# Unit 3's pieces begin after fifteen instead of twelve halves of unit 2's x products

## Chip, cores and metric

The kernel runs on one core of one Trainium2 chip. The metric is device time in microseconds (us) of one execution, lower is better. A measurement is the median of several executions; the profile is one further execution, recorded by the hardware profiler.

## What is computed

A gated linear recurrence is followed by a feed-forward block, all in float32. Cut to what matters:

```python
# q, k, v, a_re, a_im: (batch 4, heads 8, seq 768, head_dim 48)
a = (a_re + i*a_im) scaled so that its magnitude is at most 0.999
for t in range(768):                       # per batch and head, state 48 x 48, complex
    S = a[t][:, None] * S + outer(k[t], v[t])
    y[t] = q[t] @ real(S)
x = y laid out as (4*768, 8*48) = (3072, 384)
h = ((x @ w1) * (x @ w2)) @ w3             # w1, w2: 384 x 1024, w3: 1024 x 1024
out = h @ w_out                            # w_out: 1024 x 384
```

## The kernel before

The recurrence is turned into matrix products. The sequence is cut into **units** of 384 time steps, two for each batch element, eight in all (`NU = 8`), and each unit into three **chunks** of 128 steps (`UC = 3`, `C = 128`). For every unit, VectorE (DVE) and ScalarE (ACT) first prepare gates: logarithms and exponentials of the gate's magnitude, running products and sums over time (the scans, L628 and L687), sines and cosines. Gates multiply q and k into four tiles: `gR` and `k` (for k), `gA` and `q` (for q). Twelve DMA transfers (L736) then move these four into the layout that the scores need, `KL` and `QL`. The gates of unit u+1 are prepared while TensorE (PE) works on unit u. GpSimd (POOL) does nothing but check the weights and gates from the side, in a loop of its own.

PE's work on a unit's attention is a list of **pieces**:

- `tr`: three transposes of a chunk of `gR` (x = 0) or `k` (x = 1) into PSUM (`tp`, L766), then a copy to SBUF by ACT (`KT`, L768);
- `kv`: 24 products of a chunk's `KT` with v (L830), which DVE adds to the state (`T`, L836);
- `sc`: scores of four heads (L780), which DVE copies under the causal mask into `A` (L783); two pieces make a chunk;
- `y`: the chunk's output (L813), copied by ACT to `xT` (L815).

`tp`, `kv` and `y` take turns in two PSUM buffers. An odd unit such as unit 3 has these pieces:

```python
return [[("need", u), tr[0][0]], [tr[0][1]], [tr[1][0], kv[0]], [tr[1][1]], [kv[1]], sc[0], sc[1] + [y[0]],
        sc[2] + [y[1], y[2], ("end", u)]]                                    # L1196
```

The feed-forward work of the unit before is what PE does between the pieces. For unit 2 it is a list of 25 items: first 16 **halves** of the x products, in turn x @ w1 (L852 `m<-xT,w1s`, copied by ACT to `a`, L857) and x @ w2 (L852 `m<-xT,w2s`, multiplied with `a` by DVE into `ab`, L859), one pair for each of eight column blocks; then `sum` (four sums on DVE, `So`, L887); then the products with the fused output weights, in the order p1, p2, p4, p6, p7, p5, p3 (L912; a Strassen scheme of seven products, combined on DVE in L894 and by one ACT copy, L917), with `keep` (an ACT copy of part of `ab`, L878) after p7. The function that weaves the two lists is this one:

```python
def unit(u, rest, ahead):                                                    # L1226
    ...
    seq = [("begin", u)] + rest[:ahead]
    rest = rest[ahead:]
    p = pieces(u) + [[]]
    n = len(p)
    first = [i * (len(rest) - 2) // (n - 1) for i in range(n)] + [len(rest)]
    for i in range(n):
        seq += rest[first[i]:first[i + 1]] + p[i]
    return seq
```

So `ahead`, which comes from the list `AHEAD` at L432, says how many of the 25 items come before unit 3's pieces begin; the rest are spread evenly among them.

PE's order is this list. On ACT, DVE and the DMA-issuing SyncE (SP), the order is that of a planner (`run` and `fill`): after each PE item, it places gate operations of the next unit where its own clock says that they fit before the engine's next request by PE's list. [...] The gate operations of unit 4 that the prediction names are, in order: `gR` and `gA` (L717, L719, DVE), which release the `im` tile; the load of the new `im` (L512, SP); `im` times `gR` (L600, DVE); its square with a running maximum (L604, DVE, to `gZ` and `st_tan`); the logarithm of `gZ` (L586, ACT, `gZ<-gZ,consts`); a sum (L614, DVE); two exponentials and a copy (L586, ACT); a minimum (L625, DVE); and three scans (L628, DVE).

Of the kernel before, what the change touches and what calls it, by code (L numbers as in the profile page):

```python
# [376 lines left out]
def kernel(  # L377
# [51 lines left out]
    TT = S // 2  # L429
    UC = TT // C  # L430
    NU = 2 * B
    AHEAD = [0, 3, 12, 12] + [8] * (NU - 4)  # L432
    LO, HI = 32, D - 32
    PASS, WIDE, SCAN, LAND, SLACK, LATE, RING, LOOK, NEAR, EARLY = 1.17, 1.4, 1.05, 1.8, 0.7, 1.2, 8, 4.0, 4, 2
    LOOKS = 3
# [765 lines left out]
    def ffn(u, parts=1):  # L1201
        ab = [x for j in range(KF) for x in ffn_ab(u, j)]
        last = [(("o", "half")[parts - 1] if n == parts - 1 else "part", f) for n, f in enumerate(ffn_out(u, UC - 1, parts))]
        if u == 0:
            return ab + [(("part", "half")[n], f) for t in range(UC) for n, f in enumerate(ffn_out(u, t, parts))]


        def pair(*tiles):
            return [(f"p{p}", f) for p, f in zip((1, 2, 4, 6, 7, 5, 3), out_pair(tiles))]

        own, thirds = ((u, 0, False), (u, 1, False)), ((u - 1, UC - 1, True), (u, UC - 1, False))
        if u == 1:
            return ab + [("so", lambda: (out_sums(own), last[0][1]()))] + pair(*own)
        got = ab + [("sum", lambda: out_sums(own))] + pair(*own)
        if u % 2:
            return got + [("sum", lambda: out_sums(thirds))] + pair(*thirds)
        return got[:len(ab) + 6] + [("keep", lambda: keep(u))] + got[len(ab) + 6:]
# [8 lines left out]
    def unit(u, rest, ahead):  # L1226

        if u == 1:
            return [("begin", u)] + mixed([x for p in pieces(u) for x in p], rest, FILLS[1])
# [8 lines that stand above are left out]
# [175 lines left out]
    with tc.manual_schedule(engines={mybir.EngineType.PE}):  # L1413
# [30 lines left out]
        with tc.manual_schedule(engines={mybir.EngineType.Activation, mybir.EngineType.DVE, mybir.EngineType.Pool, mybir.EngineType.SP}):  # L1444
# [23 lines left out]
            for u in range(1, NU):  # L1468
                seq += unit(u, rest[HEAD:] if u == 1 else ffn(u - 1), AHEAD[u])
            seq += ffn(NU - 1)  # L1470
# [43 lines left out]
```

## Time and profile before

| | before |
|---|---|
| time, median of 3 | 552.43 us |
| range of the 3 | 551.7 to 552.54 us |
| profiled execution, its own time | 552.92 us |
| span in that profile | 551.1 us |
| PE busy | 521.0 us, 95% of the span |
| DVE busy | 372.6 us, 68% |
| ACT busy | 275.3 us, 50% |
| POOL busy | 358.0 us, 65% |
| granted PE clock, mean | 0.982 of full |

All times in the text count from the start of the span. Of the profile's views, the table of busy time gives each engine's share; the timeline lists instructions with start, duration, engine, line, operation, output and inputs, and in brackets the engine's idle time just before and what ended it; the chain of waits follows the end of the run back through whatever released each step; the table of windows gives busy time, granted PE clock (1.00 is full), DMA share and GB/s for chosen stretches. [...]the price of a piece is taken from one start to the next.

### The profile page before, as it was taken

To read this page: it belongs to the slowest core of one execution; us is meant where nothing else is said; L and a number is where in the kernel's file an instruction comes from. 1 tells how busy PE (TensorE), PEld (TensorE's weight loads), DVE (VectorE), ACT (ScalarE), POOL (GpSimd) and SP (SyncE) were. 2 spreads that over 40 slices of the span, in tenths; PEclk is the share of its full clock that TensorE was granted. 3 is DMA by queue.
4 is the path that set the end of the run, shared out by engine and by line. 5 is a ranking of instruction groups with operands and counts; after the bars stand their busy time and mean duration, and the time that the engine had idled before them with its cause. 6 is when DMAs were issued, how large, how long until landed. Compare 5 with 4: busy or idle time off the path is not lost.

```text
span 551.1 us, 13443 instructions
## 1 busy us (share of the span) xinstructions
PE 521.0 (95%) x5546; PEld 370.0 (67%) x5546; DVE 372.6 (68%) x553; ACT 275.3 (50%) x391; POOL 358.0 (65%) x425
## 2 busy tenths in 40 slices
PE   4689899989999999989999999999999999999995
PEld 2345575556756795669568985687569966795585
DVE  5999589775585677867977985687669751531152
ACT  5989766465543555746467426743494232111100
POOL 1000000188888788888998888988998888888100
PEclk9899899999999999989999999999999999999999
DMA  8997956966659835492889346935793173222001
GB/s 262 339 395 236 212 167 189 253 161 162 159 141 242 223 106 132 146 207 84 245 212 218 112 129 165 215 110 152 170 224 100 58 205 83 73 65 96 1 26 39
DMA packets 73510, 89.73 MB, mean 163 GB/s; under 512 B 31840, under 2 KB 63264, under 8 KB 72672
## 3 DMA queue, kind: packets, MB, share of 16 engines
q1 hardware_dynamic: 67360, 69.78, 48.2%
q0 software_dynamic: 6080, 19.01, 11.7%
q8 instruction: 45, 0.74, 0.6%
q14 instruction: 25, 0.20, 0.1%
HBM read 65.14 MB, written 4.72 MB: 127 GB/s over the span
## 4 chain that ended last, share of the span: by engine, by line
PE 67%; DVE 14%; DMA 8%; ACT 5%; issue 3%; SPq 1%; DVEq 0%; ACTq 0%
PE m L852 35%; PE p L912 14%; PE y L813 6%; PE sc L780 5%; PE o L948 3%; DMA im<-in_a_im_dram 2%; DMA QL<-q 2%; DMA raw<-in_w_dram 2%; DVE gZ L687 2%; PE kv L830 2%; PE tp L766 2%; ACT low L1002 1%; DVE So L887 1%; DMA out_dram<-ot 1%; ACT gZ L586 1%
## 5 line engine op out<-in xcount | busy, mean ns | idle before, releaser
L852 PE MATMUL m<-xT,w1s 128*128 128x384 f32 x384 | 134.5, 487 | 1.1 <-ACT xT L815 1.1
L852 PE MATMUL m<-xT,w2s 128*128 128x384 f32 x384 | 134.8, 487 | 0.0
L852 PEld LDWEIGHTS m<-xT,w1s 128*128 128x128 f32 x384 | 72.2, 190 | 48.9 <-ACT xT L815 1.7
L852 PEld LDWEIGHTS m<-xT,w2s 128*128 128x128 f32 x384 | 71.9, 190 | 47.8
L1069 POOL TENSOR_SCALAR look<-look 128x256 f32<-128x256 f32 (+1 forms) x84 | 86.7, 1032 | 7.3
L1050 POOL TENSOR_TENSOR seen<-seen,look 128x256 bf16<-128x256 bf16 (+1 forms) x84 | 80.9, 963 | 6.8
L859 DVE TENSOR_TENSOR ab<-m,a 128x384 f32<-128x384 f32 x64 | 35.2, 551 | 69.8 <-PE m L852 66.3
L857 ACT COPY a<-m 128x384 f32<-128x384 f32 x64 | 30.2, 473 | 95.1 <-PE m L852 95.1
L1034 POOL MEMSET seen<- 128x256 bf16 x1 | 0.3, 311 | 102.3 <-DVE w2s L1014 102.3
L1068 POOL TENSOR_SCALAR look<-look 128x256 f32<-128x256 f32 (+1 forms) x44 | 51.7, 1174 | 6.1 <-DMA look<-in_a_re_dram 2.8
L1066 POOL TENSOR_TENSOR look<-look 128x256 f32<-128x256 f32 (+1 forms) x72 | 48.6, 675 | 3.5 <-DMA look<-in_w_dram 1.7
L912 PE MATMUL p<-To,So 128*128 128x192 f32 x240 | 44.1, 332 | 0.0
L1045 POOL DMA_DIRECT2D look<-in_w_dram x56 | 33.1, 591 | 16.6 <-POOL seen L1050 16.6
L815 ACT COPY xT<-y 128x384 f32<-128x384 f32 x24 | 11.5, 478 | 60.2 <-PE y L813 60.2
L1071 POOL TENSOR_TENSOR look<-look 128x256 f32<-128x256 f32 (+1 forms) x44 | 38.1, 866 | 3.7
L912 PEld LDWEIGHTS p<-To,So 128*128 128x128 f32 x240 | 38.7, 190 | 2.2 <-issue 2.0
L768 ACT COPY KT<-tp 128x384 f32<-128x384 f32 x40 | 34.0, 857 | 11.9 <-PE tp L766 11.7
L813 PE MATMUL y<-A,V 128*32 128x128 f32 x768 | 39.8, 273 | 0.1
L783 DVE COPY_PREDICATED A<-mask,sc 128x512 f32<-128x512 uint8 x48 | 32.7, 733 | 6.4 <-PE sc L780 6.2
L813 PE MATMUL y<-QL,T 96*32 96x128 f32 x640 | 35.5, 272 | 0.8 <-issue 0.8
L813 PEld LDWEIGHTS y<-A,V 128*32 128x32 f32 x768 | 34.3, 110 | 2.1 <-issue 2.0
L1150 PE MATMUL f<-wo_s,w3s 128*128 128x384 f32 x96 | 35.6, 520 | 0.0
(129 smaller groups left out, 922.4 us busy)
## 6 DMA issues: line engine op xcount, KB each, us to landing
look<-in_w_dram POOLq DMA_DIRECT2D x56, 256.0 KB, 4.0
raw<-in_w_dram SPq DMA_DIRECT2D x6, 1024.0 KB, 10.7
KL<-gR SPq DMA_DIRECT2D x24, 192.5 KB, 4.6
KL<-k SPq DMA_DIRECT2D x24, 192.5 KB, 6.1
re<-in_a_re_dram SPq DMA_DIRECT2D x24, 192.0 KB, 4.4
im<-in_a_im_dram SPq DMA_DIRECT2D x24, 192.0 KB, 4.0
k<-in_k_dram SPq DMA_DIRECT2D x24, 192.0 KB, 8.1
q<-in_q_dram SPq DMA_DIRECT2D x24, 192.0 KB, 7.4
```

Source lines behind the costliest of these rows:

```text
L768: nc.scalar.copy(out=KT_t[u, c][:, :, :, x].rearrange("p h d f -> p f d h"), in_=tp.rearrange("p f (d h) -> p f d h", h=H))
L813: nc.tensor.matmul(out=o, lhsT=a, rhs=b, start=s0, stop=s1)
L852: nc.tensor.matmul(out=m, lhsT=w[:, j * P // WB, f, j * P % WB:j * P % WB + P], rhs=xT_t[u][:, f], start=(f == 0), stop=(f == KD - 1))
L859: nc.vector.tensor_tensor(out=ab_t[u][:, j], in0=m, in1=got[0], op=OP.mult)
L912: nc.tensor.matmul(out=m[p], lhsT=a[:, f], rhs=b[:, f], start=(f == 0), stop=(f == KH - 1))
L1045: nc.gpsimd.dma_start(out=got.bitcast(I32)[:, 0:group[2]], in_=group[1])
L1050: nc.gpsimd.tensor_tensor(out=seen[:, 0:n], in0=seen[:, 0:n], in1=x, op=OP.add)
L1066: tt(out=x, in0=x, in1=x, op=OP.mult)
L1068: ts(out=y, in0=x, scalar1=high, scalar2=None, op0=OP.is_le)
L1069: ts(out=x, in0=x, scalar1=low, scalar2=None, op0=OP.is_ge)
L1071: tt(out=x, in0=x, in1=y, op=OP.mult)
L1150: nc.tensor.matmul(out=sums[j], lhsT=w3_t[f][:, j * P:(j + 1) * P], rhs=w3_t["wo"][:, f], start=(f == 0), stop=(f == KF - 1))
```

## The change

One number changes: the fourth entry of `AHEAD`, that of unit 3, from 12 to 15.

```diff
-    AHEAD = [0, 3, 12, 12] + [8] * (NU - 4)
+    AHEAD = [0, 3, 12, 15] + [8] * (NU - 4)
```

By `unit`, 13 items are left for the weaving before, 10 after. PE's order from the thirteenth half on (halves counted from 0; `tr c,x`) becomes:

```text
before  h12 tr0,0 | h13 tr0,1 | h14 h15 tr1,0 kv0 | sum tr1,1 | p1 kv1 | p2 p4 sc0 | p6 sc1 y0 | p7 keep sc2 y1 y2 | p5 p3
after   h12 h13 h14 h15 tr0,0 | sum tr0,1 | p1 tr1,0 kv0 | p2 tr1,1 | p4 kv1 | p6 sc0 | p7 sc1 y0 | keep sc2 y1 y2 | p5 p3
```

The planner sees another list, so the built orders of ACT and DVE differ in this stretch too; those of SP and POOL are the same as before. From the thirteenth half of unit 2 to unit 3's last output (Ln, Exp, Copy: the gate operations on ACT, L586; check: L564; sq: L604; A: one mask copy, L783; scan: L628; `|` only parts the columns):

```text
ACT before  a(h12) KT KT a(h14) Ln gZ | KT KT U | Exp Exp Copy check xT check keep xT Ln xT
ACT after   a(h12) a(h14) Ln gZ | KT KT U KT KT | Exp Exp Copy check check xT keep xT Ln xT
DVE before  .. sq ab(h15) T So So So So T L614 | A A L625 U ot | A A scan scan U ot | A A scan
DVE after   .. sq ab(h15) So So So So T L614 T L625 U ot | A A scan U ot | A A scan | A A scan
```

No operation, transfer or buffer is added or removed.

## Prediction

> **What bounds the kernel now.** I read the page first, for the engine that sets the time; then the chain of waits around unit 3, for what PE hangs on there; then the timelines of PE and ACT, for the order in which things stand; last the table of windows, for the clock. The page:
>
> ```profile
> PE 521.0 (95%) x5546; PEld 370.0 (67%) x5546; DVE 372.6 (68%) x553; ACT 275.3 (50%) x391; POOL 358.0 (65%) x425
> ...
> PE 67%; DVE 14%; DMA 8%; ACT 5%; issue 3%; SPq 1%; DVEq 0%; ACTq 0%
> ```
>
> PE is the bound, so reordering its work is worth only the PE idle time that it adds or removes. After 150 us and before the last products, PE has one large hole, and it lies in the stretch that the change rearranges. PE's timeline:
>
> ```profile
> 236.60 0.49 PE L766 MATMUL tp<-ident,gR 128*128 128x128 f32 x3
> 237.02 0.88 PE L830 MATMUL kv<-vr,KT 128*32 128x48 f32 x48
> 240.27 0.55 PE L766 MATMUL tp<-ident,k 128*128 128x128 f32 x3 [2.37 <-ACT KT L768]
> ```
>
> PE waits 2.37 us for an ACT copy out of PSUM. The chain of waits for that stretch says why the copy is late:
>
> ```profile
> 230.51 4.42 DMA im<-in_a_im_dram
> ...
> 235.04 1.40 DVE im L600
> ...
> 238.12 0.09 DVE st_tan L604
> ...
> 238.23 1.25 ACT gZ L586
> 239.48 0.74 ACT KT L768
> 240.22 0.04 issue
> 240.27 0.55 PE tp L766 x3
> ```
>
> and ACT's timeline shows it standing still with work at hand:
>
> ```profile
> 234.86 0.48 ACT L857 COPY a<-m 128x384 f32<-128x384 f32 x1 [1.10 <-PE m L852]
> 238.23 1.25 ACT L586 ACTIVATE gZ<-gZ,consts 128x1152 f32<-128x1152 f32 x1 [2.89 <-DVE st_tan L604]
> 239.39 0.82 ACT L768 COPY KT<-tp 128x384 f32<-128x384 f32 x1
> 240.85 0.85 ACT L768 COPY KT<-tp 128x384 f32<-128x384 f32 x1 [0.64 <-PE tp L766]
> ```
>
> The transposes were finished at 237.09, but their copy stands behind unit 4's logarithm, and that waits for `im` (landed 234.92), its product and its square. The windows show what the hole costs beyond itself:
>
> ```profile
> 238.19:241.60 3.41, 1.33 (x9) 1.33 (x10) 3.38 (x7) 2.73 (x3) 3.24 (x3) 1.00 1.12 233
> 241.60:245.00 3.40, 3.40 (x55) 2.85 (x54) 1.62 (x3) 0.42 (x2) 2.90 (x5) 0.50 1.10 247
> 118.70:122.10 3.40, 1.93 (x11) 1.26 (x10) 3.04 (x4) 0.63 (x2) 3.00 (x4) 1.00 1.07 242
> ```
>
> First number: length; second: PE busy; third from the end: granted clock. After a window with 2.08 us idle the clock is 0.50 for 3.4 us; after one with 1.47 idle (around another hole) it stays 1.00.
>
> [...]
>
> **The change, part by part.** Prices, start to start in PE's timeline and chain: a half 1.94, three transposes 0.33, kv 0.81, a product p 1.40, both score pieces 1.25, y 1.76. Nothing is added, so the sum is over waits.
>
> *Three halves moved ahead.* PE's order up to h12 (start 228.20) is unchanged. Then h12 to h15: 4 × 1.94 = 7.76, to 235.96; tr0,0 and tr0,1: 0.66, to 236.62; p1: 1.40, to 238.02. Its operands are ready: it reads the first four column blocks of `ab` and original weights, not `So`.
>
> *When is the logarithm released?* As before, 238.23. `im` hangs on L719 (end 229.23) and three SP issues, whose order is unchanged; h13's product with `a` may start at 232.2 instead of 232.7, but DVE is in L726 until 232.63 anyway; so L600 starts with the landing at 234.92, and L604 ends at 238.2. POOL's and SP's orders do not move.
>
> *The copies, all four now behind the logarithm.* Before, two had run before it. tr1,0 needs the buffer of tr0,0: its copy runs 239.39 to 240.21, so PE starts at 240.27 as before. **The hole is 240.27 − 238.02 = 2.25 us, not gone.** The halves moved ahead put tr0,0 just where ACT stands still. Then a new wait: kv0 needs the copy of tr0,1 too, which runs next, to 240.96. PE finishes tr1,0 at 240.60 and starts kv0 at 241.02: 0.42 idle. Bounds: 0.2, if that copy were as short as its buffer hand-over allows, to 0.9, a whole copy; I take 0.42. Queued behind kv0 on PE is everything.
>
> *From 240.27 to the first scores.* tr 0.33, wait 0.42, kv0 0.81, p2 1.40, tr 0.33, p4 1.40, kv1 0.81, p6 1.40 = 6.90; the slow window, busy throughout, loses half of 3.35 = 1.67; sc0 starts at 248.84. Before, sc0 started at 247.21 and was followed by p6 (next start 1.50 later), so the same work was done at 248.71. Net **+0.13**. The idle sums alone (2.67 against 2.37) say +0.30; I take +0.15.
>
> *The sums moved ahead of T and L614 on DVE* cost nothing: the 3.2 us of sums end at 241.7, kv0 at 242; p6, the first user, is at 247. The first T then follows kv0, before kv1 wants its buffer at 246.6. The ACT copy of p1 (0.32) lies between two `KT` copies; tr1,1, which needs the second of these, comes only at 244.9.
>
> *L625 moved ahead of the mask copies.* It waits for ACT's second exponential, and the copies of `A`, which release the score banks, are queued behind it. tr1,1 ends at 245.2; its copy at 246.15; two exponentials (1.25, 1.17) at 248.5; L625 (0.98) 249.5; U and ot (0.6) 250.1; two copies (0.68 each) 251.45. PE: sc0 to 250.09, p7 to 251.5, and sc1's second piece needs the second copy at 252.1. **Spare 0.65**: hidden, but not by much. Chunk by chunk the same: scan 1.0, U and ot 0.65, copies 1.35 end at 254.45, wanted at 255.2; scan and copies end at 256.5, y2 wants them at 257.5. The last scan ends at 257.5 (before: 257.60), so unit 4's gates go on as before. `keep` and the checks wait for nothing new; xT of y2 has p5 and p3 (2.80) as cover.
>
> *What is late next where a hole goes.* The last transfer to `QL` is issued at 238.8, and these take up to 8.0 us to land, at 246.8 at most; DMA share falls from 0.95 in 245 to 246 to 0.10 in the next us. Before, sc0 at 247.21 came right after it. With p6 ahead, sc0 at 248.84 has 2 us to spare.
>
> Sum: +0.15 on the profiled execution's 552.92 us (span 551.1 and 1.8 around it). That execution lies 0.49 above the median of the runs shown, so I put the difference on the median: 552.43 + 0.15 = **552.6 us**.
>
> **The rivals.**
> - *The slow window is missed: 550.9.* [...] Then 1.67 comes back in full, since sc0 (247.2) is still behind the landing. Before, an escape was worth only some 0.8, as the transfers would have held sc0 until about 246.5. For it: the timed runs scatter by 0.84.
> - *The hole closes altogether: 550.3.* This is what more PE work ahead suggests at first sight. PE would reach sc0 at 238.02 + 6.48 = 244.5 but wait for `QL` until about 246.5, 2.3 before 248.84. Against it: the order on ACT and an unchanged landing.
> - *DVE becomes the bound of unit 3, slower: 553.7.* From L625 to the last mask copies DVE has 8.3 us without a hole, each copy wanted by PE. It decides once the delay passes 0.65. [...] For it: scans of one size range from 0.93 to 1.36. Against: most of the operations have run at the lower end.
> - *A second slow window: 554.3,* +1.67. Against: PE is busy throughout the first one, which ended it before.
>
> **How the numbers follow.** What a measurement can tell from no change is 0.2%, 1.1 us. The stall stays and nothing else changes: 0.54, its own range 552.0 to 553.0. Slow window missed: 0.22; hole closed: 0.06; these are the faster, 0.28. DVE: 0.12; second window: 0.06; slower 0.18. The range 550.6 to 553.9 takes in the likeliest, the missed window and DVE; it leaves out about 0.12 to 0.15.
>
> **What would show it.** Right: PE's timeline with a wait of about 2.2 us for `KT` L768 after p1, a second of 0.4 before kv0, four `KT` copies after the logarithm at 238.2; sc0 at 248.8; the unit's p3 done at the same time as before within 0.3. Wrong: a `KT` copy between 236.3 and 238.2; granted clock 1.00 from 241 to 245; mask copies that PE's score groups wait for; a hole before sc0 ended by DMA `QL`.

## The result and the profile after

| | before | after |
|---|---|---|
| time, median, first comparison | 552.55 us (20 executions) | 549.38 us (20) |
| ratio, 95% interval | | 0.9937, 0.9913 to 0.996 |
| ratio, second and third comparison | | 0.9975, 0.9953 to 0.9997; 0.9995, 0.9971 to 1.002 |
| mean of the three, weighted by their intervals | | **0.9969 ± 0.0013** |
| span of the profiled execution | 551.1 us | 545.4 us |

The changed kernel was faster by 0.31%, or 1.7 us, in the mean of three comparisons; the first alone showed 0.63%, the third nothing. The first and the third interval do not overlap, so the ± 0.0013, which is built from the intervals alone, is too narrow: widened to the spread of the three it is about ± 0.0033, and that just reaches 1. What does repeat is the time outside the slow clock (last experiment). Single executions of one kernel scatter by more than the effect: 75 of the kernel before ran from 545.38 to 556.67 us. (Executions in a disturbed state are left out of all ratios.)

The two profiles differ by 5.7 us of span, and less than a third of that lies where the change is. Unit 2's last `xT` copy starts at 202.41 before and 196.88 after, so 5.53 us were gained ahead of the first reordered instruction. Unit 3's last `xT` copy starts at 259.38 and 252.19: the stretch of the change is 1.66 us shorter in this pair, and the rest of the run 1.49 us longer. In both kernels PE does the same work between these two copies, so I call this "the stretch" and compare it below.

The page of the changed kernel, first the busy times, then the chain's shares:

```profile
PE 515.8 (95%) x5546; PEld 367.1 (67%) x5546; DVE 374.4 (69%) x553; ACT 274.8 (50%) x391; POOL 363.0 (67%) x425
...
PE 70%; DVE 11%; DMA 6%; SPq 4%; ACT 4%; issue 3%; DVEq 0%; ACTq 0%
```

PE is still the bound, with the same instructions. PE's timeline of the changed kernel (start, duration, instruction, in brackets the idle time ahead of it and what ended it):

```profile
231.06 1.47 PE L912 MATMUL p<-w3o,ab 128*128 128x192 f32 x8
233.97 0.55 PE L766 MATMUL tp<-ident,gR 128*128 128x128 f32 x3 [1.44 <-ACT KT L768]
234.67 0.88 PE L830 MATMUL kv<-vr,KT 128*32 128x48 f32 x48 [0.15 <-ACT KT L768]
...
239.42 1.57 PE L912 MATMUL p<-To,So 128*128 128x192 f32 x8
241.23 1.75 PE L780 MATMUL sc<-QL,KL 96*32 96x128 f32 x64 [0.24 <-issue]
```

The hole at `KT` is there, after p1, and the small one before kv0. New to me was the last line: with p6 (239.42) already ahead of them, the first scores still start with a short wait. They come 15.61 us after the first transfer to `KL` was issued (225.62); before, it was 16.06 (247.21 and 231.15). One more product was done by then, and no time was lost. ACT's timeline and the windows:

```profile
231.94 1.26 ACT L586 ACTIVATE gZ<-gZ,consts 128x1152 f32<-128x1152 f32 x1 [2.79 <-DVE st_tan L604]
233.10 1.51 ACT L768 COPY KT<-tp 128x384 f32<-128x384 f32 x2
```

```profile
231.36:234.77 3.41, 1.81 (x17) 1.28 (x18) 3.34 (x6) 2.83 (x5) 3.00 (x4) 1.00 1.07 260
234.77:238.18 3.41, 3.41 (x65) 3.32 (x66) 2.95 (x4) 1.57 (x4) 3.00 (x4) 1.00 1.08 243
```

ACT stands still behind the logarithm as before (2.79 us, 2.89 before). The window with the hole holds 1.60 us of idle PE, and no slow one follows (third number from the end 1.00): in this execution it was missed.

### The profile page after: what moved, and what is told of

Same layout as the page of the kernel before. It is cut to its first block, busy times and chain, and to the rows that moved or that the text cites. A ratio compares the mean times of both kernels' runs of the same rounds, so it can differ in the third digit from the quotient of the medians.

```text
span 545.4 us, 13443 instructions
## 1 busy us (share of the span) xinstructions
PE 515.8 (95%) x5546; PEld 367.1 (67%) x5546; DVE 374.4 (69%) x553; ACT 274.8 (50%) x391; POOL 363.0 (67%) x425
## 3 DMA queue, kind: packets, MB, share of 16 engines
q0 software_dynamic: 6080, 19.01, 12.0%
## 4 chain that ended last, share of the span: by engine, by line
PE 70%; DVE 11%; DMA 6%; SPq 4%; ACT 4%; issue 3%; DVEq 0%; ACTq 0%
PE m L852 34%; PE p L912 16%; PE y L813 7%; PE sc L780 5%; PE o L948 3%; DMA im<-in_a_im_dram 2%; DMA raw<-in_w_dram 2%; SPq L560 2%; PE kv L830 2%; PE tp L766 2%; DVE gZ L687 1%; PE f L1150 1%; DVE A L783 1%; ACT re L586 1%; DMA V<-in_v_dram 1%
## 5 line engine op out<-in xcount | busy, mean ns | idle before, releaser
L1069 POOL TENSOR_SCALAR look<-look 128x256 f32<-128x256 f32 (+1 forms) x84 | 88.5, 1053 | 7.3
L1050 POOL TENSOR_TENSOR seen<-seen,look 128x256 bf16<-128x256 bf16 (+1 forms) x84 | 74.0, 881 | 6.8
L1068 POOL TENSOR_SCALAR look<-look 128x256 f32<-128x256 f32 (+1 forms) x44 | 55.5, 1260 | 6.1 <-DMA look<-in_a_re_dram 2.9
L1066 POOL TENSOR_TENSOR look<-look 128x256 f32<-128x256 f32 (+1 forms) x72 | 54.2, 753 | 3.4 <-DMA look<-in_w_dram 1.5
L1045 POOL DMA_DIRECT2D look<-in_w_dram x56 | 33.2, 592 | 16.6 <-POOL seen L1050 16.6
L1071 POOL TENSOR_TENSOR look<-look 128x256 f32<-128x256 f32 (+1 forms) x44 | 38.6, 877 | 3.7
L783 DVE COPY_PREDICATED A<-mask,sc 128x512 f32<-128x512 uint8 x48 | 32.8, 734 | 3.7 <-PE sc L780 3.5
L780 PE MATMUL sc<-QL,KL 96*32 96x32 f32 (+3 forms) x1536 | 32.4, 235 | 2.5 <-DVE A L783 2.1
```

Of the source, the lines that this page charges most:

```text
L780: nc.tensor.matmul(out=sc[SB * g:SB * g + SB, j, s0:C], lhsT=KL[:, x * n + j, w][:, s0:s0 + SB], rhs=QL[:, x * n + j, w][:, s0:C], start=T ...
L783: last["sc", u, c, x] = nc.vector.copy_predicated(out=A[:, x * n:(x + 1) * n], data=sc, mask=mask)
L1050: nc.gpsimd.tensor_tensor(out=seen[:, 0:n], in0=seen[:, 0:n], in1=x, op=OP.add)
L1066: tt(out=x, in0=x, in1=x, op=OP.mult)
L1068: ts(out=y, in0=x, scalar1=high, scalar2=None, op0=OP.is_le)
L1069: ts(out=x, in0=x, scalar1=low, scalar2=None, op0=OP.is_ge)
```

## The experiments

Three theories. **Transfers:** the first scores wait for the twelve transfers to `KL` and `QL`, so a product ahead of them costs nothing while that wait lasts. **Hole:** the gain is in the wait at `KT` and its slow clock. **Halves:** it is in the three halves put first. Beside ratios to the kernel before, I use for each kernel's one profile two times from the first transfer's issue (to the landing of the last of the twelve, and to the first scores), the PE waits, what the slow clock took from the stretch (half of the time at 0.50) and whether that lay ahead of the first scores or behind them, and the length of the stretch. All are in us.

| kernel | last landing | first scores | waits at `KT` | wait at first scores | slow clock took | stretch |
|---|---|---|---|---|---|---|
| before | 15.6 | 16.06 | 2.37 | none | 1.7 ahead | 56.97 |
| before, again (e1) | 16.6 | 16.85 | 1.87 | 1.20 | 1.7 ahead | 57.79 |
| after | 15.3 | 15.61 | 1.44, 0.15 | 0.24 | 0 | 55.31 |
| after, again (e2) | 16.0 | 17.56 | 2.21, 0.16 | none | 1.7 ahead | 56.83 |
| tail alone (e5) | 16.5 | 16.77 | 1.68 | 1.58 | 1.7 behind | 58.40 |
| tail alone (e17) | 16.7 | 17.02 | 1.60 | 1.89 | 1.7 behind | 58.28 |
| halves alone (e6) | 19.8 | 20.11 | 4.19 | 2.16 | 1.7 ahead, 1.7 behind | 62.37 |
| before, logarithm later (e3) | 16.9 | 17.16 | 0.16 | 4.82 | 3.4 behind | 61.14 |
| after, logarithm later (e4) | 15.8 | 16.12 | none | 2.64 | 1.7 behind | 57.73 |
| one product more ahead (e7) | 16.4 | 19.12 | 2.32, 0.15 | none | 1.7 ahead | 59.48 |

In every row with a wait at the first scores, these start 0.3 us behind the last landing; in the others they start 0.5 to 2.7 us behind it.

### The two kernels again (e1, e2)

No edit.

> The kernel before, unchanged, timed against itself: it tells how far a ratio strays without any change, and whether the wait of tr1,1 and the slow clock window after it come in every execution. Theory (the gain of the change is the hole in unit 3 and the slow window that it brings): ratio 1.000 within 0.003; in its profile a hole of 1.5 to 2.4 us on PE ended by the KT copy[...]. Rival (the gain is elsewhere, for instance in units 4 to 7 or in the head of the run): the distance from the start of unit 2's h12 to the end of unit 3's y2 is the same in both kernels, and the runs differ outside it.

> The changed kernel once more, for a second profile and time. Theory: ratio 0.993 to 0.997; from h12 to y2 of unit 3 it is 1.0 to 2.0 us shorter than before, with a hole after p1 of 1.4 to 2.3 us and 0.1 to 0.5 us before kv0. Rival: the stretch is as long as before, and the gain lies outside it.

Measured: 0.9997 (0.9972 to 1.0023) and 0.9975 (0.9953 to 0.9997). The stretch of e2 is 1.0 us shorter than that of e1, but only 0.1 shorter than in the first profile of the kernel before, so the 1.0 to 2.0 that I expected are hardly there. PE's timeline of the kernel before, in this second profile, and what the view of `QL` says of its last transfers:

```profile
237.12 0.55 PE L766 MATMUL tp<-ident,k 128*128 128x128 f32 x3 [1.87 <-ACT KT L768]
245.37 1.32 PE L780 MATMUL sc<-QL,KL 96*32 96x128 f32 x64 [1.20 <-issue]
```

```profile
L736 SPq DMA_DIRECT2D QL<-q x3: 551/605/612, 235.3 to 236.5; - x3
...
DMA to landing us min/median/max: 6.1/6.6/8.6
```

This is what my one profile had not shown. PE has the hole and the slow window, and still it waits 1.20 us at the first scores. The profile names no releaser ("issue"), but the last transfer to `QL`, issued at 236.5, took 8.6 us and landed at 245.1, 0.3 us ahead of the scores. In e4 (2.64 us) and e3 (4.82 us) a DMA is named.

### The hole taken away (e3, e4)

The planner may place unit 4's logarithm only after n transposes of unit 3: n = 4 in the order of before (e3), n = 2 in that of the change (e4).

```diff
-            yield "ACT", PASS, "z1", ("sq",)
+            yield "ACT", PASS, "z1", ("sq", ("hold", u))
 ...
+                turned[0] += kind == "tr"
+                if turned[0] == n:
+                    ready["hold", 4] = 0.0
```

> PE's order of before (12 halves ahead), with one operation moved on ACT: unit 4's logarithm comes after all four KT copies of unit 3 instead of between the second and the third. Theory of the hole: no wait of tr1,1 for KT, clock 1.00 throughout, sc0 then held by the transfers to QL for up to 2 us; stretch from h12 to y2 shorter by 1.5 to 3 us, ratio 0.994 to 0.997, as good as the change. Rival, that PE's new order or DVE's new order gives the gain: the ratio stays within 0.002 of 1.

> The changed kernel (15 halves ahead), with unit 4's logarithm moved on ACT behind the first three KT copies of unit 3. Theory of the hole: no wait after p1 and none before kv0; sc0 waits for QL instead, about 2 us less than the hole and its slow window took; the stretch from h12 to y2 is 0.3 to 1.5 us shorter than in the changed kernel; ratio to before 0.991 to 0.996. Rival, that the logarithm's later start makes DVE late: mask copies that PE waits for, and no gain over the changed kernel.

Measured: e3 **1.0043** (1.0018 to 1.0068), e4 0.9993 (0.9968 to 1.0018); both lie outside what the theory of the hole expected. Closing the hole makes the kernel before slower. PE's timeline of e3, then its windows:

```profile
237.31 0.55 PE L766 MATMUL tp<-ident,k 128*128 128x128 f32 x3 [0.16 <-ACT KT L768]
247.58 2.36 PE L780 MATMUL sc<-QL,KL 96*32 96x128 f32 x64 [4.82 <-DMA QL<-q]
```

```profile
243.00:247.20 4.20, 0.00 (x0) 0.00 (x0) 0.26 (x1) 3.87 (x4) 3.61 (x6) 1.00 0.68 162
247.30:250.50 3.20, 2.92 (x66) 2.78 (x67) 1.22 (x2) 0.74 (x2) 2.70 (x5) 0.50 0.22 78
250.50:253.90 3.40, 3.40 (x44) 2.93 (x46) 1.51 (x4) 0.00 (x0) 2.99 (x4) 0.50 0.19 66
```

The hole is gone (0.16), and its time comes back as a wait of 4.82 us that the trace puts down to the transfer of q to `QL`. So the hole was covered by the transfers. One long wait is worse than two short ones here: behind it the clock stays at 0.50 for two windows, 6.6 us as shown, and they lie behind the landing, where nothing covers them, while the one slow window of e1 (1.7 us) lies ahead of it, and the first scores of e1 start 0.3 us behind the landing all the same. In the timed executions the slow clock takes 2.5 ± 1.1 us more from e3 than from the kernel before, and the time outside it differs by 0.4 ± 0.9. The theory of the hole falls for the wait itself; as I read these figures, its slow window counts only where no wait for the transfers stands behind it.

### Each part of the change alone (e5, e6, e17, e18)

The tail: `AHEAD` stays at 12, and unit 3's positions put p6 before the first scores and p7 before the second. The halves: `AHEAD` is 15, with p6 and p7 after the scores and the first output as before.

```diff
+        if u == 3:
+            first = [0, 1, 2, 4, 5, 6, 9, 10, 11, 13]   # tail alone, with AHEAD 12 (e5, e17)
+            first = [0, 1, 2, 3, 4, 5, 5, 6, 8, 10]     # halves alone, with AHEAD 15 (e6)
```

> Half of the change: 12 halves ahead and the transposes where they were before, but from p6 on the order of the change (p6 before the first scores, p7 before the second). Transfer theory (the first scores wait for the twelve transfers to KL and QL, which land about 19 us after h12 starts, so what counts is how much PE has to do until then): the first scores start no later than before although p6 stands ahead of them, and the stretch from unit 2's last to unit 3's last output copy is 1.0 to 1.6 us shorter; ratio 0.996 to 0.998. Rival, that the gain comes from moving the transposes and their copies: no gain, ratio 0.999 to 1.002.

> The other half: 15 halves ahead of the transposes as in the change, but p6 after the first scores and p7 after the first output, as before. Transfer theory: PE has as much to do before the first scores as before, so they start at the landing and the gain is gone; ratio 0.999 to 1.002, with a wait at the first scores of 0 to 2 us in the profile. Rival: the gain stays, 0.995 to 0.998.

> The tail of the change alone (12 halves ahead, p6 before the first scores, p7 before the second) a second time, side by side with the whole change on one chip. If the tail carries the gain: ratio 0.996 to 0.998 and time outside the slow clock 0.7 to 1.4 us below before. If halves and tail are both needed: 0.999 to 1.001, while the whole change stays at 0.995 to 0.998.

> The whole change a third time, beside the tail alone. Transfer theory: ratio 0.995 to 0.998, at most 1 us faster than the tail alone; in its profile the first scores at the landing or within 1.5 us after it, 15.6 to 17.6 us after the first transfer's issue, with p6 already done.

Measured: tail alone 0.998 (0.9951 to 1.0009) and **0.996** (0.9934 to 0.9985), weighted mean 0.9969 ± 0.0019; halves alone **1.0005** (0.9979 to 1.003); the whole change, beside the second tail, 0.9995 (0.9971 to 1.002), short of the 0.995 to 0.998 expected. The tail's mean is that of the whole change, and the halves bring nothing that can be seen, though e6's interval alone would leave them 0.2%. Timed on one chip, the tail (e5) is 1.9 ± 1.2 us faster than the halves (e6). PE's timeline of the tail alone (e17):

```profile
235.76 0.55 PE L766 MATMUL tp<-ident,k 128*128 128x128 f32 x3 [1.60 <-ACT KT L768]
244.41 1.32 PE L780 MATMUL sc<-QL,KL 96*32 96x128 f32 x64 [1.89 <-issue]
```

Its first scores start 17.02 us after the first issue, against 16.85 in e1, with p6 already done: the product went into the wait. But the tail's profiles do not show the gain. I expected a stretch 1.0 to 1.6 us shorter; it is 58.40 and 58.28 us, longer than in either profile of the kernel before. In both executions the hole brought no slow window, so PE came to the scores early, waited 1.58 and 1.89 us, and got its slow window there, behind the landing. What the kernel before would have taken in these two executions is not known. So it is the times, not the profiles, that speak for the tail. e6's profile caught an execution with late loads: `im` took up to 6.5 us from issue to landing, against 3.1 in the first profile of the kernel before, so the hole took 4.19 us, and a wait of 2.16 followed. It is one execution and says nothing of the halves.

### One product more (e7)

```diff
+            first = [0, 1, 2, 3, 4, 5, 7, 9, 9, 10]     # AHEAD 15: p6 p7 | first scores | keep p5 | second
```

> The change taken one product further: p6 and p7 before the first scores, p5 before the second, p3 alone at the end. Transfer theory: if the transfers still land after p6 has ended, another part of 1.4 us is gained; with the holes at KT of 1.6 to 2.7 us and half a slow window PE reaches the first scores at about 18 to 19.5 us after h12, so 0 to 1 us more than the change, ratio 0.993 to 0.997. Rival: the score banks and mask copies, with less PE work between the score groups, make PE wait for DVE; equal to the change or slower than it.

Measured: 0.9998 (0.9971 to 1.0025). The first scores came at 19.12 us without any wait, 2.7 us behind the landing: in this execution p7 found none to hide in. No gain over the change is seen, where I expected 0 to 1 us.

### The transfers made earlier (e8, e11, e12)

All but 26 of POOL's checks are left out, so its loads stop at about 220 us; e8 also has e3's edit.

```diff
+        groups = groups[:26]
```

> Unit 4's logarithm behind all four KT copies with 12 halves ahead, as in the earlier run, and all but 26 of the weight and gate checks of POOL left out, so that from about 220 us on POOL moves no data; that part of the checks is not computed. Transfer theory, in the form that the transfers wait for one another at full DMA load: without POOL's loads the last of the transfers to QL lands 2 to 4 us earlier, and the wait of the first scores falls from 4.8 to 1 to 3 us. Rival, that their landing is set by SP's issuing or by fixed delays: the wait stays at 4 to 5 us.

> The kernel before with all but 26 of POOL's checks left out (that part of the checks is not computed), as the base of the next run. Its transfers in unit 3 land earlier: expected 11 to 14 us after the first issue, below the time at which PE comes to the first scores (about 16). Ratio to the kernel before 0.985 to 0.993[...].

> The changed kernel with the same checks left out (that part is not computed). Transfer theory: the landing is no longer a floor, so p6 before the first scores has nothing to hide behind and the change brings nothing: time within 0.7 us of the previous run of this call. Rival, that the change gains by the shorter hole at KT or by DVE's order, which do not need late transfers: 1.5 to 2.5 us faster than that run.

Measured: e8 0.9909 (0.9876 to 0.9942), e11 0.9884 (0.984 to 0.9928), e12 0.9906 (0.9869 to 0.9943). With the logarithm held back, the first scores of e8 start 13.65 us after the first issue with no wait shown, where e3 waited 4.82 until 17.16. The landing comes earlier when POOL's loads are gone: 13.1 to 13.3 us after the first issue in e8, e11 and e12, 16.9 in e3. From the question for the instructions that write or read `QL`, the last line for e3, and then for e8:

```profile
DMA to landing us min/median/max: 7.2/7.9/9.2
```

```profile
DMA to landing us min/median/max: 5.1/5.7/6.0
```

With early transfers the change brings nothing: 546.63 us (e12) against 544.46 (e11), the wrong way round and more than the 0.7 us that I allowed for, though seven and six executions leave an interval of some 2 us. The theory of the transfers asks for this, but the pair cannot tell it from the theory of the hole, because without POOL's loads the hole goes too. PE's timelines, e11 and then e12:

```profile
234.00 0.55 PE L766 MATMUL tp<-ident,k 128*128 128x128 f32 x3 [0.32 <-ACT KT L768]
```

```profile
236.89 0.49 PE L766 MATMUL tp<-ident,gR 128*128 128x128 f32 x3
```

### The transfers made later (e13 to e16)

Three transfers more after unit 3's twelve, in four kernels: before, tail alone, whole change, halves alone.

```diff
             move(QL, (A, q), s)
+            if u == 3:
+                for f in range(KD):
+                    nc.sync.dma_start(out=KL[f::2 * KD], in_=R[:, f])
```

> The kernel before with three more transfers (a second copy of the first three to KL, the same bytes) after unit 3's twelve, as the base of the next three runs. The last of them should land about 2.4 us later (three at 0.8 us), so the first scores wait at 18 to 20 us after the first issue in nearly every execution; ratio 1.001 to 1.005.

> The same three transfers, with 12 halves ahead and only the tail of the change (p6 before the first scores, p7 before the second). Transfer theory: with the landing surely behind PE's work, p6 is hidden whole: 1.0 to 1.6 us faster than the base of this call. Rival, that the halves ahead make the gain: same as the base within 0.7 us.

> The same three transfers with the whole change. Transfer theory: as with the tail alone, 1.0 to 1.6 us faster than the base. If hole and slow window count besides, faster than the tail alone by another 0.5 to 1 us; if they are hidden by the wait for the transfers, equal to it.

> The same three transfers with 15 halves ahead, but p6 after the first scores and p7 after the first output as before. Transfer theory: no gain, within 0.7 us of the base. Rival: 1 to 2 us faster than the base.

Measured: 1.0085 (1.0056 to 1.0114), 1.012 (1.004 to 1.0201, six executions), 1.0078 (1.0052 to 1.0104), 1.0102 (1.0073 to 1.0132). In times: 556.27, 556.97, 555.09 and 556.35 us. The whole change is 1.2 us ahead of its base, the halves alone 0.1 behind; both point as expected, but the intervals overlap. The tail, expected 1.0 to 1.6 us ahead, came out 0.7 behind, and its six executions decide nothing. Outside the slow clock (split as in the last experiment) the whole change takes 1.5 ± 1.3 us less than the halves alone, about the price of one product. The profiles say more. PE's timelines at the first scores, halves alone (e16), then the whole change (e15):

```profile
248.05 2.36 PE L783 MATMUL sc<-QL,KL 96*32 96x128 f32 x64 [5.53 <-DMA KL<-gR]
```

```profile
247.89 2.33 PE L783 MATMUL sc<-QL,KL 96*32 96x128 f32 x64 [2.03 <-DMA KL<-gR]
```

The added transfer is the one that PE waits for. In both the scores start at the same place, 19.58 and 19.54 us after the first issue, but the whole change has p6 behind it by then and waits 2.03 instead of 5.53. (The rest of that 3.5 is hole, 2.21 us in e15 and 1.64 in e16, and slow clock, 1.7 us in e15 and none in e16 before the wait: again the wait absorbs them.) What I had not expected is the price: three transfers cost the kernel before 4.7 us. Of that, 3.2 ± 1.0 lie outside the slow clock, as the last landing is later (19.3 us after the first issue in e15 and e16), and 1.5 ± 1.1 in it.

### Two ways to go further (e9, e10)

e9 fills the hole with work at hand: p1, p2 and p4 before the second chunk's transposes, p6 and p7 before the first scores. e10 puts three products of no use into the hole of the changed kernel.

```diff
+            return seq + [h15, need, t00, t01, sums, p1, p2, p4, t10, kv0, t11, p6, kv1, p7, *sc0, kept, p5, *sc1, *sc2, p3]
```

```diff
+        if (u, c, x) == (3, 1, 0):
+            w = ps_m.tile([P, TT], FP, tag="mm", name="warm")
+            for _ in range(3):
+                nc.tensor.matmul(out=w, lhsT=ident, rhs=xT_t[u - 1][:, 0], start=True, stop=True)
```

> The changed kernel with the hole filled by its own work: p1, p2 and p4 stand together before the second chunk's transposes, p6 and p7 before kv1 and the first scores, p5 before the second, p3 at the end. Transfer theory (the landing of the transfers, 15.6 to 17.2 us after the first of them is issued, is a floor under the first scores, and PE time idle or at half clock before it is regained only if useful work stands there): hole at KT under 1 us, no slow window from it, first scores at the floor with a wait of 0 to 2 us; 1 to 2 us faster than the change, ratio to before 0.991 to 0.996. Rival: the score groups, with less PE work between them, wait for DVE's mask copies and take it back; ratio 0.996 to 1.001.

> The changed kernel with three products of no use (1.94 us of PE, their result is never read) in the hole before tr1,0. [...] If the slow window costs what it seems to (1.7 us in about half of the executions, no transfer wait behind it in this order): mean slow-clock loss over a run lower by 0.5 to 1.5 us than in the changed kernel, ratio to before 0.992 to 0.996. Rival, that PE then only waits at the first scores for the transfers: no gain over the change, with the wait at the first scores longer by about 1.5 us.

Measured: e9 **0.9954** (0.9931 to 0.9978), e10 **0.9951** (0.9924 to 0.9979). Both are clearly faster than before, 548.31 and 548.56 against 550.95 us. Against the change's mean of 0.9969 neither is told apart. e9's PE timeline shows what was meant:

```profile
238.00 1.57 PE L912 MATMUL p<-To,ab 128*128 128x192 f32 x8 [1.09 <-ACT U L917]
240.87 0.55 PE L766 MATMUL tp<-ident,k 128*128 128x128 f32 x3 [0.17 <-ACT KT L768]
245.09 1.32 PE L780 MATMUL sc<-QL,KL 96*32 96x128 f32 x64
```

The long wait at `KT` has become 1.09 us before p4, whose buffer waits for p1's copy; no slow window follows (granted clock 1.00 from 234 to 244 us), and the first scores start at 16.39 us, 0.3 behind the landing, with p6 and p7 done. e10 is the odd one: idle time turned into useless work did no harm and perhaps good, which fits a slow window worth something in this order, but its interval does not show it.

### The timed executions, split

Each timed execution also has its mean granted clock, and (1 − clock) × span is what the slow clock took from the whole run. The differences to the kernel before on the same chip, in us:

| timed kernels | all | outside the slow clock | in it |
|---|---|---|---|
| whole change (e2, e18) | −1.23 ± 0.76 | −0.95 ± 0.55 | −0.28 ± 0.84 |
| tail alone (e5, e17) | −1.31 ± 0.78 | −0.52 ± 0.57 | −0.79 ± 0.76 |
| halves alone (e6) | +0.61 ± 0.99 | +0.28 ± 0.92 | +0.33 ± 0.94 |
| all eight with p6 before the first scores and no other load (e2, e4, e5, e7, e9, e10, e17, e18) | −1.37 ± 0.44 | −0.85 ± 0.34 | −0.52 ± 0.45 |

The gain of the whole change outside the slow clock is the same in both comparisons, −0.9 and −1.0; what differs is the part in it, −0.9 and +0.3. The tail's gain is clear as a whole but not as a part: e17 is 0.2 ± 0.9 below before outside the slow clock, where I expected 0.7 to 1.4. The first comparison cannot be split, as it has no clocks of the kernel before.

## Why the prediction was wrong

**The step that failed** is "From 240.27 to the first scores", where the start of the first scores, 247.21 before, was taken as set by PE's own work, and p6 ahead of them was charged in full: "sc0 starts at 248.84 ... the same work was done at 248.71. Net +0.13". The sum was right only where PE comes to the scores after the landing. In the profile that I had, it came 0.5 us after it. I had bounded the landing at 246.8, 15.65 us after the first issue, from the longest issue-to-landing time in that one execution. In e1 and both tails the scores waited until 16.8 to 17.0. So more than half of p6's 1.4 us was free: −0.85 ± 0.34 outside the slow clock. I used the transfers only as a cap on what a closed hole could bring, and did not ask what they hide.

Two comparisons say that it was the old order which I had wrong. In the changed kernel's second profile, which has the hole and the slow window as forecast, the first scores start 20.51 us after h12; the forecast was 20.64. (In the first profile, without the slow window, it was 18.56.) In the kernel before they start 19.01 us after h12 in the profile that I read, but 19.83 in e1, and there p6 still has to follow.

This accounts for some 1.4 us with the slow clock's part. The first comparison showed 3.2; the rest did not come back in the second and third, and its cause stays open.

**The hole stays** was right: 1.44 us in the profile after and 2.21 in e2, forecast 2.25. (ACT's 2.89 us of idle before were not all with a ready copy behind: the transposes ended at 237.09, so it was ready for the last 1.14.) **The wait before kv0** was right as well: kv0 starts 0.70 and 0.71 us after the transposes, forecast 0.75. (The brackets show 0.15 and 0.16 because they count from a longer end of the transposes, 0.55 us after their start, than the 0.33 of the forecast.)

**The logarithm is released as before** held: 7.08 and 6.56 us after the first issue before, 6.32 and 7.07 after. What I took as a fixed time moves by 0.7 between executions of one kernel, and with it the hole (2.37 and 1.87 us before, 1.44 and 2.21 after) and, in the two profiles of the change, the slow window.

**The slow window can be missed** was right: the granted clock stayed at 1.00 behind the hole of 1.44 us in the profile after, and fell to 0.50 behind that of 2.21 us in e2. How often it is missed was not shown. Its rival's number, 550.9, is close to the mean gain of 1.7 us, but that is luck: it names the smaller part, −0.52 ± 0.45, and charges p6 in full.

**The hole closes altogether, 550.3,** was wrong in sign for the old order (e3, 1.0043): the wait for `QL`, 4.82 us, took the hole's place, and two slow windows followed it. In the new order (e4) nothing was gained: PE waited 2.64 us at the scores, and a slow window followed.

**DVE's mask copies** stayed hidden in the change: in the profile after, no score group after the first waits for them, as the sum with its spare of 0.65 us said. The 553.7 of that rival was my estimate, and no run shows it.

## What to carry to other kernels

Where the engine that bounds a kernel meets transfers, find in several profiles whether it arrives before or after them: a tie in one profile (no wait in the first of the kernel before) was a wait of 1.20 us in the next (e1). Work put ahead of that meeting was free here for as long as the wait lasted, more than half of p6's 1.4 us; a stall closed ahead of it was worth nothing here, and cost 0.4% (e3) when its idle time moved to where nothing covered the slow clock behind it. When several moves ride on one number, try each alone: here the three halves that the change is named after did nothing visible (1.0005), and by the times the gain went with the product that slipped ahead with them.

## What the hardware showed unexpectedly

A wait of 4.82 us of PE was followed by two windows at half clock (e3, the 6.6 us shown), although PE was busy for 2.92 of the first 3.20 us; the wait of 2.37 us in the kernel before was followed by one. The length of the wait does not settle it: the hole of 4.19 us in e6 was followed by only one, with PE busy for 3.02 of its 3.41 us. Nor does the idle time in a window alone say whether a slow one follows: 1.60 us at `KT` left the clock at full (after, e17), 1.58 us at the first scores was followed by half clock (e5).

The transfers to `QL` took 7.2 to 9.2 us to land beside POOL's loads in e3 and 5.1 to 6.0 without them in e8. From the first issue to the last landing it was 13.1 to 13.3 us in the three runs without these loads, and 15.3 or more in every row of the table.
